# Planning a PE order with latencies and durations as traced per kind of matmul, and grouping PV by where the exponential was computed

## The chip, the cores and the metric

One core of one Trainium2 chip. The metric is the device time of one execution in microseconds. Most executions of a kernel agree within 0.3%; some fall into a slower state with a lower granted TensorE clock. Those are listed and left out of every comparison. Ratios are the mean time of one kernel's fast runs over that of the other's fast runs of the same rounds, so they are not quite the ratio of the medians that are quoted. The classes are faster, same and slower, with the line at 2%.

## The reference

Two attentions over the same sequence length, side by side in one program. Attention A is the heavy one: 16 query heads of width 28 share one key and one value head. Attention B looks back at 8 positions only.

```python
def _A_ref(x, wq, wk, wv, wo):           # x: 1 x 2048 x 448, H = 16, Dh = 28
    q = ...                               # x @ wq, split in 16 heads
    k = x @ wk; v = x @ wv                # one head each
    scores = jnp.einsum("bhqd,bkd->bhqk", q, k) * (Dh ** -0.5)
    p = _softmax(scores, axis=-1)         # 16 x 2048 x 2048 exponentials
    o = jnp.einsum("bhqk,bkd->bhqd", p, v)
    return ... @ wo

def _B_ref(x, wqkv, wo):                  # the same shapes; W = 8, dil = 2
    qkv = ...                             # x @ wqkv
    # keys and values at positions pos - 0, 2, ..., 14, with a mask
    logits = jnp.einsum("bhsd,bhswd->bhsw", q, kg) * scale
    attn = _softmax(...)
    return ... @ wo

return jnp.concatenate([a, b], axis=-1)
```

## The kernel before

ScalarE computes A's exponentials from PSUM, two or three score banks of 512 columns at a time (410 instructions). VectorE computes another 60 banks by a polynomial on the bits. TensorE (PE) makes the scores (QK), multiplies exponentials by values (PV), and fills what time is left with everything else: the projections of both attentions, B's logit sums and transposes, the output projections, and filler matmuls that are there to keep PE dense. QK and PV are *tiled*: two or three 32-row matmuls (QK) or four 32-column ones (PV) run side by side. The rest is called full-array work here; a projection over the 448 inputs takes three matmuls of 128 rows and one of 64. A second form of QK, called kz here, uses keys padded with zeros and the full array.

The kernel's order of instructions is not written down by hand. A greedy planner simulates the engines with a duration for each operation and latencies between engines, and emits each engine's list. What matters here is the rule that stops full-array work in time for the next QK. `H` is when ScalarE would run dry in the plan, `limit` is when PE must be free:

```python
class Sched:
    LAT = 0.13
    ...
    QKT = 0.32
    EPS = 0.03
    ...
        def ready(o):
            ...
                lat = self.LAT if d.eng != o.eng or d.dsem else (0.0 if o.eng == "pe" else self.OWN)
    ...
            H = tE["act"] + sum(o.dur for (_, o) in cand["act"] if o.ring)
            ...
            if e == "pe":
                rq = min((r for (r, o) in cand["pe"] if o.ring), default=None)
                if rq is not None and T > 14:
                    limit = max(rq, H - self.QKT - self.LAT)
                    ...
                    if limit is not None and not o.ring and T + o.dur > limit + self.EPS:
                        nxt = limit if nxt is None else min(nxt, max(limit, T + 0.02))
                        continue
```

And the way PV groups were formed. A PV group takes one bank from each of four heads. Banks that VectorE computes come late, and were put at the head of their list, so that they mixed with ScalarE's:

```python
            while late and late[0][0] <= n // 2:
                for x in late.pop(0)[1]:
                    quads[x[0][:2]][x[0][3]].insert(0, x)
            for u in us:
                js = quads[u[:2]]
                while all(js):
                    g.pv_group([x.pop(0) for x in js])
    ...
    def pv_group(self, grp):
        ...
        o = a("pe", 0.33, pv, ...)
        if last:
            o.deps.update(g.pvs[qd])
        elif not first:
            o.deps.add(g.pvs[qd][0])
```

Durations are constants or a rule: `t_mm(n) = 0.02 + 0.42e-3 * max(n, 100)`, which is 0.235 us for 512 columns.

## Time and profile before

| what | before |
|---|---|
| time, median of 3 runs | 475.45 us (475.41 to 476.12) |
| span of the profiled run, granted clock | 473.0 us, 0.999 |
| ScalarE busy | 451.8 us of 473.0 |
| first exponential starts, last ends | 12.31, 464.17 us |
| from the last exponential's end to the end | 8.8 us |
| waits between exponentials | 15.3 us |

How to read it: the page's busy share says which engine is full, and here it is ScalarE. The last row is not from the page. It is counted from the starts of the exponentials in the trace, as the prediction below works out.

### The profile page before, as it was taken

How to read it: one execution, taken by the hardware profiler on the slowest of the kernel's cores; microseconds unless marked ns; L12 is line 12 of the kernel's file. 1: busy time of each engine (PE TensorE's matmuls, PEld its weight loads, DVE VectorE, ACT ScalarE, POOL GpSimd, SP SyncE). 2: the span in 40 equal slices, each digit the busy share in tenths (PEclk: the TensorE clock that was granted, in tenths of full speed). 3: DMA queues.
4: the chain of work that ended last, by engine and by line, in shares of the span. 5: the costliest groups of instructions: out<-in, count | busy, mean ns of one | idle time of the engine just before them, and what ended most of it. 6: DMA issues, size and time to landing. Idle time of an engine off the chain costs nothing.

```text
span 473.0 us, 8630 instructions
## 1 busy us (share of the span) xinstructions
PE 436.5 (92%) x3629; PEld 173.3 (37%) x3684; DVE 365.2 (77%) x600; ACT 451.8 (96%) x430; POOL 12.5 (3%) x30
## 2 busy tenths in 40 slices
PE   8999999999899999999999999999999899989886
PEld 3433233343343424333343334322443244424333
DVE  4454878987888887897959688788968968786864
ACT  3999999999999999999999999999999999999993
POOL 8100000000000000000000000000000000000000
PEclk9999999999999999999999999999999999999999
DMA  9790022000220302000320302000310123013001
GB/s 193 147 219 3 2 87 89 11 1 10 80 89 21 108 29 89 11 10 2 98 79 30 108 14 86 10 11 15 111 63 11 50 79 97 12 48 119 11 0 60
DMA packets 41718, 27.34 MB, mean 58 GB/s; under 512 B 17090, under 2 KB 41520, under 8 KB 41680
## 3 DMA queue, kind: packets, MB, share of 16 engines
q1 hardware_dynamic: 39600, 25.25, 18.4%
q10 hardware_dynamic: 1776, 0.81, 0.7%
q0 software_dynamic: 304, 0.73, 0.6%
q8 instruction: 29, 0.48, 0.4%
q14 instruction: 9, 0.07, 0.1%
HBM read 17.60 MB, written 5.52 MB: 49 GB/s over the span
## 4 chain that ended last, share of the span: by engine, by line
ACT 70%; PE 26%; DVE 1%; DMA 1%; issue 1%; ACTq 0%
ACT expT L785 69%; PE ps L768 6%; PE ps L936 6%; PE ps L813 4%; PE ps L714 2%; PE ps L766 2%; PE ps L952 2%; DMA d_x<-in_A_wq_dram 1%; PE ps L643 1%; ACT e_t L1013 1%; PE ps L895 1%; PE ps L678 1%; PE ps L413 1%; PE ps L1045 1%; PE ps L728 0%
## 5 line engine op out<-in xcount | busy, mean ns | idle before, releaser
L785 ACT ACTIVATE expT<-ps 128x1024 bf16<-128x1024 f32 (+1 forms) x410 | 444.3, 1213 | 6.0 <-PE ps L768 4.5
L768 PE MATMUL ps<-qT,kT 32*128 32x512 bf16 x800 | 118.7, 384 | 14.5 <-ACT expT L785 11.2
L813 PE MATMUL ps<-expT,v_aug 128*32 128x512 bf16 x964 | 99.3, 389 | 0.1
L846 DVE TENSOR_SCALAR d_x<-ps 128x512 f32<-128x512 f32 x60 | 41.5, 691 | 45.2 <-PE ps L768 39.2
L766 PE MATMUL ps<-qT,kz 128*128 128x512 bf16 x189 | 58.6, 382 | 12.1 <-ACT expT L785 8.5
L768 PEld LDWEIGHTS ps<-qT,kT 32*128 32x128 bf16 x800 | 29.2, 90 | 80.8 <-ACT expT L785 51.8
L1038 PE MATMUL ps<-ident,prod 128*112 128x128 bf16 x512 | 48.5, 226 | 0.2 <-issue 0.2
L813 PEld LDWEIGHTS ps<-expT,v_aug 128*32 128x32 bf16 x964 | 24.9, 93 | 61.6 <-issue 58.1
L1038 PEld LDWEIGHTS ps<-ident,prod 128*112 128x112 bf16 x512 | 36.7, 129 | 21.8 <-issue 17.9
L936 PE MATMUL ps<-xT_B,wqkv 128*112 128x512 bf16 (+1 forms) x128 | 44.1, 407 | 0.2
L978 DVE TENSOR_TENSOR stage<-qTB,kTB 112x1024 bf16<-112x1024 bf16 x64 | 42.2, 679 | 2.2 <-PE ps L987 2.1
L1032 DVE TENSOR_TENSOR prod<-Vsh,a_n 128x896 bf16<-128x896 bf16 x64 | 37.4, 615 | 4.5 <-PE ps L1038 4.4
L858 DVE SCALAR_TENSOR_TENSOR dexp<-d_u,d_x 128x1024 int16<-128x1024 f32 x30 | 36.5, 1217 | 0.1
L856 DVE SCALAR_TENSOR_TENSOR d_u<-d_u,d_x 128x1024 f32<-128x1024 f32 x30 | 36.4, 1213 | 0.1
L854 DVE SCALAR_TENSOR_TENSOR d_u<-d_x 128x1024 f32<-128x1024 uint16 x30 | 36.3, 1210 | 0.1
L987 PEld LDWEIGHTS ps<-ones,stage 112*128 112x128 bf16 x512 | 20.4, 96 | 12.7 <-issue 7.6
L987 PE MATMUL ps<-ones,stage 112*128 112x4 bf16 x512 | 24.6, 167 | 0.1
L766 PEld LDWEIGHTS ps<-qT,kz 128*128 128x128 bf16 x224 | 14.3, 97 | 27.0 <-ACT expT L785 22.2
L936 PEld LDWEIGHTS ps<-xT_B,wqkv 128*112 128x112 bf16 (+1 forms) x128 | 14.2, 127 | 22.5 <-issue 18.3
L714 PE MATMUL ps<-xT_A,wq 128*128 128x512 bf16 (+1 forms) x60 | 19.9, 385 | 1.3 <-DVE v_aug L693 0.6
L952 PE MATMUL ps<-wqv,xT_B 128*128 128x448 bf16 x64 | 19.4, 358 | 0.0
L1045 PE MATMUL ps<-wo_B,oT 112*128 112x448 bf16 x64 | 18.1, 356 | 0.8 <-DVE oT L1041 0.8
(101 smaller groups left out, 310.2 us busy)
## 6 DMA issues: line engine op xcount, KB each, us to landing
Vsh<-v_scratch SPq DMA_DIRECT2D x16, 896.0 KB, 4.7
v_scratch<-Vst SPq DMA_DIRECT2D x16, 112.0 KB, 1.7
out_dram<-outB SPq DMA_DIRECT2D x16, 112.0 KB, 1.7
out_dram<-outA SPq DMA_DIRECT2D x14, 112.0 KB, 1.7
wqkv<-in_B_wqkv_dram SPq DMA_DIRECT2D x1, 672.0 KB, 4.7
stage<-in_A_x_dram ACTq DMA_DIRECT2D x1, 448.0 KB, 3.4
wo_B<-in_B_wo_dram SPq DMA_DIRECT2D x4, 98.0 KB
wo<-in_A_wo_dram SPq DMA_DIRECT2D x4, 98.0 KB
```

The costliest lines, as they stand in the source:

```text
L766: r = e.matmul(g.bank(b0 + i), g.kz[:, j, 128 * tb:128 * tb + 128], g.qT[:, sc % 2, t, :], start=True, stop=True)
L768: r = e.matmul(g.bank(b0 + i), g.kT[32 * j:32 * j + 32, 128 * tb:128 * tb + 128], g.qT[32 * j:32 * j + 32, sc % 2, t, :], start=True, stop ...
L785: x = a("act", t_exp(w), lambda e, b0=b0, w=w, n=n: e.activation(g.expT[:, n % ERING, 0:w], g.ps[:, 512 * b0:512 * b0 + w], ACT.Exp, scale ...
L813: x = e.matmul(g.bank(PVBANK, p0=32 * j, p1=32 * j + 32), g.v_aug[:, w, tb, :], src, start=first, stop=last, tile_position=(0, 32 * j))
L846: o = a("dve", t_dve_ps(512), lambda e: e.tensor_scalar(out=xx[:, 512 * h:512 * h + 512], in0=g.bank(bank), scalar1=-128.0 * A2, scalar2=1 ...
L856: a("dve", t_dve_1x(1024), lambda e: e.scalar_tensor_tensor(out=v, in0=u, scalar=EQ * F * F, in1=lo, op0=ALU.add, op1=ALU.mult), R=["d_u"] ...
L858: a("dve", t_dve_1x(1024), lambda e: e.scalar_tensor_tensor(out=out, in0=v, scalar=EL / F ** 3, in1=xx, op0=ALU.mult, op1=ALU.subtract), R ...
L936: a("pe", t_mm(512), lambda e, u=u, t=t, kt=kt, w=w: e.matmul(g.bank(u.bank, p1=KC), g.wqkv[64 * (kt // 3):, kt, w * D + KC * t:w * D + KC ...
L978: op = a("dve", t_dve_2x(1024), lambda e, t=t, qv=qv, kv=kv: e.tensor_tensor(out=g.prodT[0:KC, t, :, :], in0=qv, in1=kv, op=ALU.mult), R=R ...
L987: r = e.matmul(g.bank(u.bank, 128).rearrange("p (h w) -> p h w", w=WIN)[:, 4 * t:4 * t + 4, w], g.prodT[0:KC, t, w, :], g.ones4[:, :], sta ...
L1032: a("dve", t_dve_2x(2 * D), lambda e, qr=qr, Vv=Vv, av=av: e.tensor_tensor(out=g.prod2[:, 2 * qr:2 * qr + 2, :].rearrange("p w (d h) -> p ...
L1038: a("pe", 0.09, lambda e, u=u, t=t, w=w: e.matmul(g.bank(u.bank, 128, 128 * t, p1=KC), g.prod2[:, w, KC * t:KC * t + KC], g.ident[:, :], s ...
```

## The change

Its intent: let the planner know what the trace shows. One latency of 0.13 becomes one per engine. A switch from full-array to tiled work costs 0.09 us and is reserved. QK and PV are 0.315 us, four logit sums 0.1 instead of 0.2, a transpose 0.056 instead of 0.09. The 512-column projections keep 0.235. Four banks of VectorE form a PV group of their own, and the 16 groups of a quad may run in any order.

```diff
+    LATS = {"pe": 0.12, "act": 0.18, "dve": 0.08}
+    MODE = 0.09
+    NPV = 3
-    QKT = 0.32
+    QKT = 0.315
...
+    def lat(self, d):
+        if d.dsem or d.eng not in self.LATS:
+            return self.LAT
+        return self.LATS[d.eng] + (self.MODE if d.eng == "pe" and not d.tiled else 0)
...
-                    limit = max(rq, H - self.QKT - self.LAT)
+                    limit = max(rq, H - self.QKT - 0.12)
...
-                    if limit is not None and not o.ring and T + o.dur > limit + self.EPS:
+                    if limit is not None and not o.ring and not (o.pv and npv > self.NPV) and T + o.dur > limit + self.EPS - (0 if o.tiled else self.MODE):
...
-                elif (o.full and area(T) < (self.FULL[o.full] if T + 0.03 + 0.216 * o.full + self.LAT <= H + self.EPS else self.LOW)
+                elif (o.full and area(T) < (self.FULL[o.full] if T + 0.22 * o.full + 0.2 <= H + self.EPS else self.LOW)
...
+                if o.tiled and not mode:
+                    o.dur += self.MODE
+                mode = o.tiled
...
-                    quads[x[0][:2]][x[0][3]].insert(0, x)
+                    dqs[x[0][:2]][x[0][3]].append(x)
+                    if all(dqs[x[0][:2]]):
+                        g.pv_group([y.pop(0) for y in dqs[x[0][:2]]])
...
-        o = a("pe", 0.33, pv, ...)
-        if last:
-            o.deps.update(g.pvs[qd])
-        elif not first:
-            o.deps.add(g.pvs[qd][0])
+        o = a("pe", 0.315, pv, ...)
+        o.deps.update(g.evacs)
...
-                a("pe", 0.2, lgs, ...)
+                a("pe", 0.1, lgs, ...)
...
-                a("pe", 0.09, lambda e, u=u, t=t, w=w: e.matmul(
+                a("pe", 0.056, lambda e, u=u, t=t, w=w: e.matmul(
```

(Cut: the new fields of an operation, the same latencies used at bank releases and evacuations and in the limits for VectorE's work and for filler, kz planned at 0.22 us for each bank, and a table of offload positions that is rewritten with the same values.)

More of the change, by code (lines that the diff above doesn't have):

```diff
@@ L38 @@
 A2 = SCALE * 1.4426950408889634
-OFF_AT = {q: (0, 2, 4, 6, 7, 9) if q == 99 and q < 15 else (0, 2, 5, 7) for q in range(1, 16)}
+OFF_AT = {q: (0, 2, 5, 7) for q in range(1, 16)}
+OFF_AT.update({q: (0, 1, 3, 4, 6, 7, 9, 10) for q in ()})
 LATE = 2
@@ L50 @@
                  "kids", "start", "end", "seq", "waits", "signal", "count", "vc", "ninc", "claims", "idx",
-                 "dense", "fill", "full", "opt", "alone", "lock", "ring")
+                 "dense", "fill", "full", "opt", "alone", "lock", "ring", "tiled", "pv")
     def __init__(self, eng, dur, emit, pr, rel, name):
@@ L71, in __init__ @@
         self.ring = False
+        self.tiled = False
+        self.pv = False
         self.lock = isinstance(dur, Lock) or (eng == "gp" and emit is not None)
@@ L144, in run @@
         recent = []
+        mode = False
         locks = {"dve": 0.0, "gp": 0.0}
@@ L152, in ready @@
             for d in o.deps:
-                lat = self.LAT if d.eng != o.eng or d.dsem else (0.0 if o.eng == "pe" else self.OWN)
+                lat = self.lat(d) if d.eng != o.eng or d.dsem else (0.0 if o.eng == "pe" else self.OWN)
                 t = max(t, d.end + lat)
@@ L166, in use_ready @@
                         return None
-                    t = max(t, d.end + self.LAT)
+                    t = max(t, d.end + self.lat(d))
             return t
@@ L183, in run @@
                     n = sum(1 for (_, o) in cand["act"] if o.ring)
-                    limit = max(r1, H + (0.9 if n < 1 else 0) - self.QKT - 2 * self.LAT - 0.69)
+                    limit = max(r1, H + (0.9 if n < 1 else 0) - self.QKT - 0.2 - 0.69)
             if e == "pe":
@@ L187, in run @@
                 if rq is not None and T > 14:
-                    limit = max(rq, H - self.QKT - self.LAT)
+                    limit = max(rq, H - self.QKT - 0.12)
+            npv = sum(1 for (r, o) in cand[e] if o.pv and r <= T) if e == "pe" else 0
             for (r, o) in cand[e]:
@@ L254, in run @@
                     o.dense += 512 - o.use.spare
-                elif (o.full and area(T) < (self.FULL[o.full] if T + 0.03 + 0.216 * o.full + self.LAT <= H + self.EPS else self.LOW)
-                      and all(d.start is not None and d.end + self.LAT <= T for d in o.opt)):
+                elif (o.full and area(T) < (self.FULL[o.full] if T + 0.22 * o.full + 0.2 <= H + self.EPS else self.LOW)
+                      and all(d.start is not None and d.end + self.lat(d) <= T for d in o.opt)):
                     o.deps.update(o.opt)
-                    o.dur = 0.03 + 0.216 * o.full
+                    o.dur = 0.22 * o.full
+                    o.tiled = False
                     o.dense = 512 * o.full
@@ L263, in run @@
                     if T > 14 and area(T) > self.LOW:
-                        o.fill = max(0, min(o.fill, int((H - self.LAT - T - o.dur + self.EPS) / 0.22)))
+                        o.fill = max(0, min(o.fill, int((H - 0.12 - self.MODE - T - o.dur + self.EPS) / 0.22)))
                     o.dur += 0.22 * o.fill
                     o.dense += 512 * o.fill
+                if o.tiled and not mode:
+                    o.dur += self.MODE
+                mode = o.tiled
                 if o.dense:
@@ L286, in run @@
                     self.bank_last[b] = set(o.use.ops)
-                    self.bank_free_t[b] = max(x.end for x in o.use.ops) + self.LAT
+                    self.bank_free_t[b] = max(x.end + self.lat(x) for x in o.use.ops)
             for k in o.kids:
@@ L744, in a_loop @@
         assert len(units) == NU
-        g.last_exp, g.pvs = {}, {}
+        g.last_exp, g.pvs, g.evacs = {}, {}, []
         quads = {(sc, t): [[] for _ in range(4)] for sc in range(4) for t in range(4)}
+        dqs = {k: [[] for _ in range(4)] for k in quads}
         pair, late = [], []
@@ L771, in a_loop @@
             box = []
-            o = a("pe", 0.32, lambda e, qk=qk, box=box: qk(e, box=box), R=[("kT", tb // 4) for (_, _, tb, _) in us] + [("qT", sc % 2, t) for (sc, t, _, _) in us],
+            o = a("pe", 0.315, lambda e, qk=qk, box=box: qk(e, box=box), R=[("kT", tb // 4) for (_, _, tb, _) in us] + [("qT", sc % 2, t) for (sc, t, _, _) in us],
                   W=[("ring", slot)], pr=-50)
             box.append(o)
-            o.ring = True
+            o.ring = o.tiled = True
             o.full = len(us) if len(us) > 1 else 0
@@ L807, in pv_group @@
         qd = grp[0][0][:2]
-        n = len(g.pvs.setdefault(qd, []))
-        first, last = n == 0, n == 15
+        all_pv = g.pvs.setdefault(qd, [])
+        box = []
         def pv(e):
+            order = [o.seq for o in all_pv]
+            first, last = box[0].seq == min(order), box[0].seq == max(order)
             for (_, _, tb, j), _, src, w in grp:
@@ L815, in pv @@
             return x
-        o = a("pe", 0.33, pv, R=sorted({y[1] for y in grp}) + sorted(
-            {(k, y[3], y[0][2] // 4) for k in ("v_aug", "v_aug1") for y in grp}), W=["pv"] if first or last else [], pr=-40, dense=700)
-        if len(g.pvs) == 1 and first:
-            o.claims = [PVBANK]
-        if last:
-            o.deps.update(g.pvs[qd])
-        elif not first:
-            o.deps.add(g.pvs[qd][0])
-        g.pvs[qd].append(o)
-        if last:
+        o = a("pe", 0.315, pv, R=sorted({y[1] for y in grp}) + sorted(
+            {(k, y[3], y[0][2] // 4) for k in ("v_aug", "v_aug1") for y in grp}), pr=-40, dense=700)
+        o.tiled = o.pv = True
+        box.append(o)
+        if qd == (0, 0):
+            o.claims = [PVBANK]
+        o.deps.update(g.evacs)
+        all_pv.append(o)
+        if len(all_pv) == 16:
             g.a_quad_end(*qd)
@@ L866, in a_quad_end @@
         last = sc == 3 and t == 3
+        evacs = []
         hv = 2 if last else 1
@@ L873, in a_quad_end @@
             p0 = -30 if last else -1
-            a("dve", t_dve_ps(w), lambda e, cs=cs: e.transpose(out=g.PV_T[:, t % 2, cs], in_=g.bank(PVBANK)[:, cs]),
-              R=["pv"], W=kk("PV"), pr=-30)
+            o = a("dve", t_dve_ps(w), lambda e, cs=cs: e.transpose(out=g.PV_T[:, t % 2, cs], in_=g.bank(PVBANK)[:, cs]),
+                  W=kk("PV"), pr=-30)
+            o.deps.update(g.pvs[sc, t])
+            evacs.append(o)
             pt = g.PV_T[:, t % 2, :].rearrange("p (b e) -> p b e", e=32)
@@ L884, in a_quad_end @@
               R=[("oN", x) for x in keys], W=[("oTn", t, x) for x in keys], pr=p0)
+        g.evacs = evacs
         pr = end + 20
@@ L989, in lgs @@
                     return r
-                a("pe", 0.2, lgs, R=[("prodT", t), "ones4"], W=[u], use=u, pr=pr)
+                a("pe", 0.1, lgs, R=[("prodT", t), "ones4"], W=[u], use=u, pr=pr)
         par = (k // 2) % 2
```

## The prediction

> **What bounds the kernel now.** The page's busy times first, then the exponential's row by shape, then the chain of waits in order of time, then single starts in the trace.
>
> ```profile
> PE 436.5 (92%) x3629; PEld 173.3 (37%) x3684; DVE 365.2 (77%) x600; ACT 451.8 (96%) x430; POOL 12.5 (3%) x30
> ...
> ACT 70%; PE 26%; DVE 1%; DMA 1%; issue 1%; ACTq 0%
> ...
> L785 ACT ACTIVATE expT<-ps 128x1024 bf16<-128x1024 f32 (+1 forms) x410 | 444.3, 1213 | 6.0 <-PE ps L768 4.5
> ```
>
> ScalarE is the bound: 410 exponentials of two or three score banks. The page gives only 6.0 us of idle before them, which would cap any gain at 1.3%. That figure is too small. A waiting exponential overlaps the tail of the one before, so part of each wait is inside "busy". The chain of waits shows it better:
>
> ```profile
> 110.12 1.49 PE ps L936 x5
> 112.93 1.27 PE ps L936 x4
> 114.58 31.11 ACT expT L785 x29
> ...
> 446.52 12.65 ACT expT L785 x12
> ```
>
> Where only ScalarE is on the chain it makes 12 exponentials in 12.65 us, 1.054 each. From starts in the trace, the undisturbed step is 1.331 us after a three-bank exponential (145 of them) and 0.904 us after a two-bank one (264): 145 x 1.331 + 264 x 0.904 + one short = 432.1 us. The 8 small exponentials of the other attention take 0.43 each (3.4) and the 4 column ones about 0.1 each. The phase runs from 12.31 to 464.17, 451.9 us, so some **15.3 us** are waits. PE pieces as above stand in the chain wherever the next scores came late.
>
> Taking each start minus the one before minus its undisturbed step, I sorted the 15.3 us by what stood ahead of the score matmuls (QK): 9.6 us in 54 waits where a tiled QK stood behind full-array work (6.5 of it behind the projections wqkv and wq); 2.0 us in 13 waits at triples of the untiled form of QK (kz); 2.0 us in 11 waits where QK was ready and the exponential waited for something else; 0.4 us at kz pairs; 1.3 us in scatter below 25 ns. The two largest of the 2.0 us, at 88 and 97 us (0.64 and 0.81), are a full ring of exponentials: PV groups that contain a VectorE bank were held until VectorE's last step ended at 97.53, and QK stood behind PV.
>
> **The time budget of one QK.** After a two-bank exponential PE has 0.904 us. The trace has 0.171 us from its end to the QK that reuses its banks, and 0.442 us from that QK's start to the next exponential: 0.613 us, so 0.29 us is left for whatever PE is still doing.
>
> ```profile
> 459.22 0.39 PE L763 MATMUL ps<-warm 128*128 128x512 bf16 x1 [0.23 <-ACT expT L785]
> 459.54 0.39 PE L768 MATMUL ps<-qT,kT 32*128 32x512 bf16 x3
> 459.86 0.40 PE L813 MATMUL ps<-expT,v_aug 128*32 128x512 bf16 x4
> 460.19 0.61 PE L766 MATMUL ps<-qT,kz 128*128 128x512 bf16 x2
> ```
>
> Starts differ by 0.32 for each tiled group and 0.32 for a full-array matmul before QK, though full-array matmuls follow each other at 0.216 to 0.227. So a switch into a tiled mode costs about 0.09 us.
>
> **What the Trainium skill says.** (1) "TensorEngine Tiling (Array Packing)", Tiling Modes, Key Properties: changing the tiling mode drains TensorE. The trace agrees: 0.322 for filler to QK against 0.22 filler to filler; 0.285 for the output projection to QK against 0.189 within it. (2) "TensorE: Matmul & The Clock Gate", Single matmul latency: (398 + N) / 2.4 ns warm, 379 ns at N = 512; the trace has 384 to 389. Granted clock is 0.999, so the clock gate plays no part before. (3) "ScalarE: Activation LUTs", What ACT_TABLE_LOAD costs (its paragraph on ACTIVATE): 186 ns + 0.833 N, back-to-back ones overlapping by about 93 ns, hence 946 ns at N = 1024; the trace steps at 904, and that is used. (4) "Perfetto Trace Analysis", Identifying the Most-Contended Engine: occupancy is a fair measure for ScalarE, not for TensorE. Here 96% hides a third wait in "busy", so I used starts.
>
> **The change, part by part.** No exponential, bank, matmul of the result or offload is added or removed; the orders give the same 410 exponentials with 60 banks on VectorE. Only the planner's numbers change, and the grouping of PV.
>
> *Latencies and the switch.* Before, the planner let full-array work run to 0.13 + 0.32 = 0.45 us before ScalarE would run dry, with one latency of 0.13 each way: 0.58 in all, and no switch. Measured are 0.613 and 0.09 on top, so each filled gap is short by 0.12. The new numbers are 0.18 + 0.315 + 0.12 = 0.615 and 0.09, which is what the trace shows. Of the 9.6 us, 5.3 lie within the first 0.12 us of the waits and should go. The other 4.3 us come from projections: the planner takes 0.235 for a 512-column matmul, and that is not changed; the trace has 0.26 to 0.31 for wqkv and 0.225 to 0.32 for wq, 0.03 to 0.08 too little each. They sit ahead of 83 tiled QKs in the new order against 69. But gaps are filled in steps of 0.235, so most have room for 0.03 to 0.1. Estimate: 2.7 of 9.6 us stay; **-6.9**.
>
> *kz triples.* A triple takes 3 x 0.226 and ends 0.862 us after its start; with 0.171 that is 1.03 against 0.904, hence the 0.13 us each. The planner now asks 0.22 x 3 + 0.2 = 0.86, and the orders show triples fall from 14 to 4. **-1.4** of 2.0.
>
> *VectorE's four banks as one group.* One PV group in 16 waits for VectorE instead of up to four mixed ones, and exponentials' buffers no longer hang on it. **-1.5** of 2.0. Pairs and scatter stay (1.7).
>
> *The end.* The last block of the other attention closes the kernel:
>
> ```profile
> 466.05 1.00 PE ps L1038 x18
> 467.06 0.82 PE ps L895 x4
> 467.88 0.61 DVE outA L905
> 468.49 0.67 DVE oT L1041
> 469.21 0.94 PE ps L1045 x4
> ```
>
> After the last QK the order had 29 of its transposes, the new one 9; at 0.056 us these are 1.1 us. They now all precede the last output matmuls, and oT is evacuated before outA instead of after both, so the final block starts about 0.6 x 2 earlier. **-1.1**.
>
> *The head, which gets worse.*
>
> ```profile
> 0.81 15.57 SPq L578 DMA_TRANSPOSE xT_A<-in_A_x_dram  x12
> ...
> 11.94 0.35 PE ps L768 x3
> 12.31 1.46 ACT expT L785
> ```
>
> The first QK waits for nothing but k and q. The old order had ten key projections ahead of it, the last needing the sixth transpose. The new one has twelve, the last two needing the seventh and eighth. Transposes are issued 1.30 us apart, so the eighth goes out at 9.9 and, by its landing record, is in at 13.58. The first QK must follow: 13.58 + 0.06 + 0.31 for that matmul = 13.95 instead of 11.94. The first exponential moves from 12.31 to about 14.3: **+2.0**, and as ScalarE is the bound all of it counts. The planner believes in faster transposes (0.9 us apart).
>
> Sum: -6.9 - 1.4 - 1.5 - 1.1 + 2.0 = -8.9, so 475.45 - 8.9 = **466.5 us**, -1.9%.
>
> **The rivals.** (a) *Only the page's idle counts* (6.0 us): 475.45 - 6.0 - 1.1 + 2.0 = 470.4. For it: that is what the profile prints. Against: the starts, where 49 waits of over 0.1 us follow two-bank exponentials alone. (b) *The projections take the wait over*: with their 0.235 unchanged and 83 instead of 69 of them ahead of QK, the 4.3 us stay whole and some new waits come: 468 to 470. For it: more QKs sit right behind them (57 for wqkv against 45). Against: the 0.09 is now kept free at each. (c) *PE becomes the bound.* Adding the traced steps over the new order gives 409 us of PE work from first to last QK against 432 of exponentials (411 in the old one); PE isn't the bound on average, but with 95% load a stricter limit can push PV back until the seven exponential buffers are full. 4 us of that would make it 470. (d) *All waits go and the head is harmless*: 475.45 - 14 - 1.1 = 460.
>
> **Range and chances.** The head (+2.0) and the end (-1.1) are read from the orders and sure to about 0.5. The waits left are the wide term: 5.4 of 15.3 expected, 2.5 to 10 plausible. That gives 462.0 to 471.5 around 466.5. The 2% line is at 465.9 and lies 0.6 us under the centre, so faster and same are near even, same a little ahead. Slower would need a new stall of 18 us, of which nothing speaks but an unforeseen dependency or a lost clock: 0.02.
>
> **What would show it.** The first exponential at about 14.3 us behind a wait for the transpose: head right; at 12.3: wrong. Exponentials: steps over 0.904 and 1.331 summing to 3 to 7 us, the rest behind wqkv and wq; if the sum stays over 10, the latencies were not the cause or (b) or (c) holds. No exponential with QK ready and a long wait: the grouping worked. From the last exponential to the end 7.7 us instead of 8.8. PEclk must stay at 9 in all slices; a slice lower makes the prediction wrong, and so does an idle PE that waits for VectorE's four-bank group.

## The result, and the profile after

| | before | after |
|---|---|---|
| fast runs, first batch | 475.31 to 476.12 us (4) | 469.65, 468.96 us |
| slow runs | none | 477.92, 478.23 us (clock 0.974, 0.975) |
| median of all 4 | 475.43 us | 473.78 us |
| ratio of fast runs, 95% interval | | 0.9868 (0.9844 to 0.9892): same |

The fast runs are 6.1 us shorter. The profiled run after is a fast one, so the two traces compare. The page of the changed kernel, its busy row, its chain of waits by engine, and the exponentials' row (busy and mean ns, then idle before them):

```profile
span 467.6 us, 8711 instructions
PE 441.1 (94%) x3700; PEld 171.0 (37%) x3700; DVE 363.5 (78%) x600; ACT 449.7 (96%) x430; POOL 12.8 (3%) x30
ACT 68%; PE 28%; SPq 1%; DMA 1%; DVE 1%; issue 0%
L804 ACT ACTIVATE expT<-ps 128x1024 bf16<-128x1024 f32 (+1 forms) x410 | 441.8, 1211 | 3.9 <-PE ps L787 3.4
```

ScalarE is still the bound and still 96% busy. Its idle time before exponentials fell by 2.1 us and its busy time by 2.1; neither figure is the 6.0 us by which the waits fell, counted below. The chain's PE share did not fall, 26% before and 28% now. That is the first sign that many waits are still there, only shorter.

Where the 5.4 us of span went, from starts in the two traces:

| | before | after | difference |
|---|---|---|---|
| first exponential starts | 12.31 | 14.68 | +2.4 |
| first exponential to end of last | 451.9 | 445.4 | -6.5 |
| end of last exponential to end of kernel | 8.8 | 7.6 | -1.2 |

The waits between exponentials, sorted as in the prediction (us, and in brackets how many waits of over 25 ns):

| the exponential waits because | before | predicted | after |
|---|---|---|---|
| tiled QK stood behind full-array work | 9.6 (54) | 2.7 | 6.2 (64) |
| tiled QK stood behind tiled work | 0 | 0 | 0.6 (4) |
| kz triple | 2.0 (13) | 0.6 | 0.4 (2) |
| kz pair | 0.4 (5) | 0.4 | 0.3 (5) |
| scores ready, exponential waits for something else | 2.0 (11) | 0.5 | 0.3 (8) |
| scatter below 25 ns | 1.3 | 1.3 | 1.4 |
| sum | 15.3 | 5.5 | 9.2 |

Every row but the first did what was predicted, to 0.6 us. The first gave 3.4 of the expected 6.9.

One thing is missing from this count: the waits beside the four small column operations that ScalarE runs between exponentials. Before, there are two, 0.6 us in all (at 17 and 29 us, both behind full-array work); after, none of note. With them the sums are about 15.9 and 9.3 us, and the fall of 6.6 us fits the 6.5 us that the phase lost. In later tables e6 and e12 lack 1.4 us each for the same reason, e7 and e10 0.3.

This stretch of the chain of waits, in order of time (start, length, what), shows the head of the changed kernel:

```profile
5.99 1.26 SPq L596
7.29 5.89 DMA xT_A<-in_A_x_dram
13.18 0.05 issue
13.23 1.08 PE ps L661 x3
14.31 0.53 PE ps L787 x5
```

The first QK (L787) comes directly after three key projections (L661) that had waited for a transposed load. And the end, from the same view:

```profile
459.12 1.24 PE ps L921 x6
460.36 0.36 PE ps L836 x4
...
462.81 0.76 PE ps L921 x3
...
464.11 0.60 DVE outA L931
464.72 0.59 DVE outB L1074
```

B's transposes and the copy of their result, which stood between A's last PV and the last output before, are gone from it.

What remains in the middle looks like this in PE's timeline (start, length, operation, shapes, count):

```profile
47.27 0.39 PE L787 MATMUL ps<-qT,kT 32*128 32x512 bf16 x2
47.59 1.21 PE L962 MATMUL ps<-xT_B,wqkv 128*112 128x512 bf16 x4
48.72 0.39 PE L787 MATMUL ps<-qT,kT 32*128 32x512 bf16 x3
```

Four projections hold PE from 47.59 to the QK at 48.72, that is 1.13 us. The plan had 4 x 0.235 + 0.09 = 1.03. The exponential of that QK came 0.14 us late. So the switch is reserved now, but the projections overrun it.

The experiments below treat this as one matter of the projections' duration. The starts in the trace say more: from each of the four to what follows it takes 0.260, 0.216, 0.309 and 0.352 us. The last of the four has 64 rows, and the step from a 128-row to a 64-row matmul costs about 0.09 us as well (0.309 against 0.216 here; 0.285 against 0.189 for the 448 columns of wqv). It is a second switch, and the plan reserves only the one into tiled work. Of the 3.4 us of waits behind wqkv and wq, 2.4 (18 waits) follow projections with such a 64-row matmul among them and 1.0 (12 waits) follow projections without one, though the QKs of the two sorts are about as many (42 and 41). No run plans this switch by itself.

### The profile page after: what moved, and what is told of

Same layout as the page of the kernel before. It is cut to its first block, busy times and chain, and to the rows that moved or that the text cites. A ratio compares the mean times of both kernels' runs of the same rounds, so it can differ in the third digit from the quotient of the medians.

```text
span 467.6 us, 8711 instructions
## 1 busy us (share of the span) xinstructions
PE 441.1 (94%) x3700; PEld 171.0 (37%) x3700; DVE 363.5 (78%) x600; ACT 449.7 (96%) x430; POOL 12.8 (3%) x30
## 4 chain that ended last, share of the span: by engine, by line
ACT 68%; PE 28%; SPq 1%; DMA 1%; DVE 1%; issue 0%
ACT expT L804 67%; PE ps L787 6%; PE ps L836 5%; PE ps L962 4%; PE ps L785 2%; PE ps L1064 2%; SPq L596 1%; DMA xT_A<-in_A_x_dram 1%; PE ps L732 1%; PE ps L921 1%; PE ps L431 1%; PE ps L978 1%; PE ps L696 1%; ACT e_t L1039 1%; PE ps L1013 1%; PE ps L661 0%
## 5 line engine op out<-in xcount | busy, mean ns | idle before, releaser
L787 PE MATMUL ps<-qT,kT 32*128 32x512 bf16 x838 | 124.3, 384 | 9.9 <-ACT expT L804 8.1
L836 PE MATMUL ps<-expT,v_aug 128*32 128x512 bf16 x964 | 95.9, 389 | 1.0 <-ACT expT L804 1.0
L787 PEld LDWEIGHTS ps<-qT,kT 32*128 32x128 bf16 x838 | 30.6, 91 | 84.3 <-ACT expT L804 58.9
L785 PE MATMUL ps<-qT,kz 128*128 128x512 bf16 x186 | 55.6, 382 | 4.7 <-ACT expT L804 4.6
L1064 PE MATMUL ps<-ident,prod 128*112 128x128 bf16 x512 | 43.8, 224 | 0.1
L1064 PEld LDWEIGHTS ps<-ident,prod 128*112 128x112 bf16 x512 | 34.8, 129 | 16.7 <-issue 12.7
L732 PE MATMUL ps<-xT_A,wq 128*128 128x512 bf16 x64 | 21.3, 386 | 0.5 <-DVE qT L755 0.5
L1013 PEld LDWEIGHTS ps<-ones,stage 112*128 112x128 bf16 x512 | 18.0, 96 | 7.6 <-issue 3.6
L1013 PE MATMUL ps<-ones,stage 112*128 112x4 bf16 x512 | 20.7, 167 | 0.0
L785 PEld LDWEIGHTS ps<-qT,kz 128*128 128x128 bf16 x186 | 12.1, 98 | 20.7 <-ACT expT L804 18.3
```

The lines of the kernel that those rows point to most:

```text
L785: r = e.matmul(g.bank(b0 + i), g.kz[:, j, 128 * tb:128 * tb + 128], g.qT[:, sc % 2, t, :], start=True, stop=True)
L787: r = e.matmul(g.bank(b0 + i), g.kT[32 * j:32 * j + 32, 128 * tb:128 * tb + 128], g.qT[32 * j:32 * j + 32, sc % 2, t, :], start=True, stop ...
L836: x = e.matmul(g.bank(PVBANK, p0=32 * j, p1=32 * j + 32), g.v_aug[:, w, tb, :], src, start=first, stop=last, tile_position=(0, 32 * j))
L1013: r = e.matmul(g.bank(u.bank, 128).rearrange("p (h w) -> p h w", w=WIN)[:, 4 * t:4 * t + 4, w], g.prodT[0:KC, t, w, :], g.ones4[:, :], sta ...
L1064: a("pe", 0.056, lambda e, u=u, t=t, w=w: e.matmul(g.bank(u.bank, 128, 128 * t, p1=KC), g.prod2[:, w, KC * t:KC * t + KC], g.ident[:, :], ...
```

## The experiments

Each edit is against the changed kernel. All results were correct. The kernel before ran beside them on each chip, at 475.48 to 475.62 us median. Three theories were to be told apart. *Spacing*: what remains is where the plan's durations are shorter than the trace's. *Head*: what is missing was lost in the first 15 us. *Reshuffle*: a different order is a different draw, and differences of a microsecond mean nothing.

### e1_head: the head alone undone

Only four key projections are moved, behind the third group of scores; nothing else changes place.

```diff
+    def k2_later(self):
+        pe = s.seqs["pe"]
+        k2 = [o for o in pe if o.use is not None and o.use.name == "K2"][:4]
+        ring = [o for o in pe if o.ring]
+        rest = [o for o in pe if o not in k2]
+        n = rest.index(ring[2]) + 1
+        s.seqs["pe"] = rest[:n] + k2 + rest[n:]
+        # (cut: positions and start times made consistent)
```

> The changed kernel with only the four key projections of chunk 2 moved behind the third group of scores; every other instruction keeps its place. Theory (the head waits for a transposed load): the first exponential comes at 12.2 to 12.5 us instead of 14.68, and all of the 2.3 us stays saved to the end, so 466.5 to 467.3 in the fast state. Rival (the head is harmless, the time is made up for later, or the score wait only moves to the next exponential): the time stays within 0.6 us of the changed kernel's fast 469.3.

Measured: 468.75, 468.48, 468.77 us fast, one slow at 477.51; ratio 0.9855. Their mean of 468.7 is 0.6 us under the changed kernel's 469.3, not 2. The profiled run was a slow one, so its times are not compared with others, but the order of events is read. VectorE's timeline there (the last bracket is the idle time before, and what ended it):

```profile
12.12 0.42 DVE L701 TENSOR_TENSOR d_u<-kT 128x512 bf16<-128x512 bf16 x1
16.89 0.69 DVE L699 CAST kT<-ps 128x512 bf16<-128x512 f32 x1 [4.35 <-PE ps L689]
```

VectorE's next instruction was the copy of exactly those four projections, so it sat 4.35 us (in this slow run; in a fast one that time is not known) and the keys behind it came late. The first exponential was earlier, the following ones waited. The head theory falls as it was put: the 2.4 us at the first exponential are not 2.4 us at the end. The traces of before and after say the same: by the 17th exponential the changed kernel is only 0.7 us behind (32.91 against 32.21), because the kernel before had 1.5 us of waits in its first 40 us (2.0 with those beside the column operations) and the changed one 0.3. But e1 brings a wait of its own, so it does not tell what a late first exponential costs when nothing else changes; e9 below does.

### e2_numbers_only and e3_grouping_only: the two halves of the change

e2 keeps the new numbers and takes the old PV grouping; e3 the other way round.

```diff
 e2: -                    dqs[x[0][:2]][x[0][3]].append(x) ...
     +                    quads[x[0][:2]][x[0][3]].insert(0, x)       (and the old pv_group)
 e3: -    LATS = {"pe": 0.12, "act": 0.18, "dve": 0.08}; MODE = 0.09; QKT = 0.315 ...
     +    LATS = {}; MODE = 0.0; QKT = 0.32                            (and the old durations)
```

> The planner's new numbers with the old grouping of PV. It has the late head too (twelve key projections before the first scores) and no work of the other attention after the last scores. Theory (the two parts save different waits): waits of ready scores for a full ring come back, 1.5 us or more in a few waits of over 0.3 us, while waits behind full-array work stay near the changed kernel's 6.2 us; 470.5 to 473. Rival (the grouping does nothing of its own): 469 to 470 and no such wait.

> The new grouping of PV with the planner's old numbers. Its head is the old one (first exponential near 12.3 us). Theory: ring waits under 0.5 us instead of 2.0, but waits behind full-array work at 9 to 11 us and at kz triples 1.5 to 2.5 us as before; 472 to 474.5. Rival (the grouping is the whole gain and the numbers do nothing): 467 or less. On the slow state: this order has 238 untiled score matmuls against 186 in the changed kernel; if slow runs come from a lower granted clock where the array is less filled, none of its runs is slow.

Measured: e2 471.93 to 472.22 us (3 fast, 3 slow at 480.14 to 495.13), ratio 0.9926 (0.9912 to 0.9941). e3 473.22 to 474.04 us (5 fast, 1 slow at 489.07), ratio 0.9957 (0.9944 to 0.9971). Times 475.5 these are -3.5 and -2.0 us. Both times lie in the ranges of their theories. Together -5.5, against -6.3 for both at once (1 - 0.9868): nearly additive. Both profiled runs were slow ones, so the waits that the theories name could not be read, and e3's slow run contradicts its guess on the slow state. The grouping is worth about what the prediction gave it (-1.5); the numbers are what fell short.

### e5_changed_again: the changed kernel, unchanged, in a later batch

> The changed kernel as it is, to have its fast time and its share of slow runs beside the next three on one chip. Fast runs near 469.3; one to four of six slow, at 477 to 480, and if a slow one is profiled, its clock is halved in one block of time that begins between 10 and 20 us and nowhere else. Rival for the slow state: the halved clock is spread over the kernel.

Measured: 469.41, 468.66, 469.0 us fast; 491.27, 478.03, 477.69 us slow; ratio 0.9858 (0.9841 to 0.9875). The trace sorts into the same classes to 0.01 us (6.22 us in 64 waits behind full-array work). So these waits came out the same in two runs of one order, and can be argued about one by one.

### e9_control: a reshuffle that means nothing

```diff
-    EPS = 0.03
+    EPS = 0.031
```

> The changed kernel with the planner's margin moved by a nanosecond (0.030 to 0.031 us): a control for what a mere reshuffle of the order is worth. Reshuffle theory (the gains of the wider margin and of the longer projections are luck of the order): 467.0 to 471.0 us, that is, it differs from the changed kernel's 469.0 by over 0.8 us one way or the other, and waits behind full-array work move by over 1.5 us from 6.2. Spacing theory (they are gains from planning what the trace shows): 468.5 to 469.8 us, and behind full-array work 5.5 to 7.0 us.

Measured: 468.19 and 469.01 us fast, 478.18 and 476.34 slow; ratio 0.9855 (0.9837 to 0.9873). Behind full-array work 6.0 us in 60 waits. The waits moved by 0.2 us, as spacing has it; the mean of the two runs, 468.6, is 0.4 us from 469.0, though the lower run is 0.3 us under spacing's range. As a control it is weak: the nanosecond hardly changed the order. What stands ahead of a score matmul is the same as in the changed kernel for 1001 of 1024 (for e7 for 530), and nearly all of the rest lies between 299 and 326 us. So what a real reshuffle is worth was not measured, and reshuffle stays open for differences of a microsecond between e4, e7, e10 and e11.

The trace of the lower run shows something else: the same three key projections stood before the first QK, but the transposed loads landed earlier (the eighth at 12.77 us, not 13.79) and its first exponential started at 13.57 us instead of 14.68. So the head itself varies by 1.1 us from run to run. And with the order so nearly equal, those 1.1 us were kept: the 17th exponential starts at 31.79 instead of 32.91, and the last ends at 458.54 instead of 460.04.

### e4_margin and e7_proj: what is left, reserved in two ways

e4 keeps 0.13 us more free ahead of every QK. e7 plans the 512-column projections with a spacing like the traced one.

```diff
 e4: -    EPS = 0.03
     +    EPS = -0.10
 e7: -    return 0.02 + 0.42e-3 * max(n, 100)
     +    return {512: 0.265, 448: 0.208}.get(n, 0.02 + 0.42e-3 * max(n, 100))
```

> The changed kernel with the planner told to end work 0.13 us earlier ahead of each group of scores (EPS from 0.03 to -0.10). Theory (the remaining 6.2 us of waits behind full-array work are the projections' and other steps that run 0.03 to 0.1 us longer than planned, and lateness carried over): these waits fall to 2 to 3.5 us, the time to 465 to 467.5. Rival (PE is the bound; what is kept free ahead of the scores is missing elsewhere): waits move to other kinds and the sum stays at 8 us or more, 468 to 471.

> The changed kernel with 0.265 instead of 0.235 us planned for every 512-column full-array matmul (448 columns stay at 0.208). Theory (half of the waits left are these matmuls running longer than planned): waits behind projections fall from 3.4 to 1.5 us or less, those behind other work stay; the planner itself now leaves 1.2 us more of gaps, so 467 to 469.3. Rival (the waits are lateness that is carried over from earlier work, whatever stands last): the waits behind projections stay above 2.5 us.

Measured: e4 467.49 to 470.4 us in 5 runs, ratio 0.9857 (0.9837 to 0.9876); behind full-array work 4.3 us in 48 waits, but kz triples are back at 2.4 us. Its theory (2 to 3.5 us, 465 to 467.5) missed, but for the lowest run's time; the sum of waits is still some 8 us and the other four runs lie at 468 to 471, as its rival said. Its two longest runs, 469.53 and 470.4, show clocks of 0.996 and 0.993. e7 467.49 to 467.68 us in 4 runs, ratio 0.9831 (0.9818 to 0.9844); behind full-array work 3.65 us in 45 waits. Behind the projections wqkv and wq it is 1.3 us where the changed kernel has 3.4. The exponentials' row and the chain of e7:

```profile
ACT 72%; PE 22%; DVE 2%; SPq 2%; DMA 1%; issue 0%
L804 ACT ACTIVATE expT<-ps 128x1024 bf16<-128x1024 f32 (+1 forms) x410 | 441.9, 1226 | 2.0 <-PE ps L787 1.2
```

The idle time before exponentials halves, from 3.9 to 2.0, and PE's part in the chain falls from 28% to 22%. So the waits behind the projections are a matter of their planned duration. (0.265 is an average that covers the 64-row step too.) But the sum of waits falls only from 9.2 to 8.3: kz triples and pairs come back with 3.0 us where the changed kernel has 0.8. And of the 1.5 us that e7 gains over e5, only 0.6 lie between the first exponential and the last (444.8 against 445.3); the rest is an earlier head (13.37 against 14.63): this order has 11 key projections ahead of the first QK, not 12.

### e6_mode0 and e12_mode0_old_short: is it the switch?

e6 takes the switch away and leaves all other new numbers. e12 does the same, and also plans the two short kinds as long as before.

```diff
 e6 and e12: -    MODE = 0.09
             +    MODE = 0.0
 e12 too:    -                a("pe", 0.1, lgs, ...
             +                a("pe", 0.2, lgs, ...
             -                a("pe", 0.056, lambda e, u=u, t=t, w=w: e.matmul(
             +                a("pe", 0.09, lambda e, u=u, t=t, w=w: e.matmul(
```

> The changed kernel with the planner's cost of a switch into a tiled mode set to zero (MODE 0.09 to 0), its latencies kept. Theory (the switch is most of what was missing: 0.09 of 0.12): waits behind full-array work go back up from 6.2 to 9 us or more, mean wait from about 0.10 to about 0.17 us, fast time 471 to 474 although its head is early. Rival (the latencies did it, the switch matters little): waits behind full-array work stay at 5.5 to 7, and with the early head the time is 467.5 to 469.

> The run without the switch (MODE 0, 478.2 us) once more, but with the two short kinds of full-array matmul planned as long as before: 0.09 us for a transpose of the other attention and 0.2 for a group of four logit sums, where the trace has 0.056 and 4 x 0.025. Theory that the old over-long durations had kept the room that the switch needs: waits of scores behind these two kinds fall from 3.4 us (23 waits) to under 1, waits behind full-array work in all from 14.4 to 9 to 12 us, time 473.5 to 476 us. Rival, that without the switch the other new latencies are what costs: waits behind the projections and fillers stay, the short kinds don't matter, and the time stays at 477 to 479 us.

Measured: e6 478.16 to 478.34 us (4 fast, one slow at 489.83), ratio 1.0056 (1.0042 to 1.0069). It is slower than the kernel before, and 4 us over its theory's range: the sign was foreseen, the size was not. e12 471.5 to 472.31 us in 4 runs, ratio 0.9927 (0.991 to 0.9944), 1.2 to 2.0 us better than its theory's range and far from the rival's. The chain of waits of e6, by engine and by line, then of e12:

```profile
PE 50%; ACT 46%; SPq 1%; DMA 1%; DVE 1%; issue 0%
ACT expT L804 45%; PE ps L787 12%; PE ps L836 8%; PE ps L962 6%; PE ps L1064 6%; PE ps L785 4%; PE ps L732 3%; PE ps L978 2%; PE ps L1013 2%; PE ps L431 1%; PE ps L1071 1%; SPq L596 1%; DMA xT_A<-in_A_x_dram 1%; PE ps L408 1%; PE ps L696 1%; PE ps L746 1%
```

```profile
ACT 75%; PE 21%; SPq 1%; DMA 1%; DVE 1%; issue 1%
ACT expT L804 74%; PE ps L787 5%; PE ps L962 5%; PE ps L836 3%; PE ps L732 2%; SPq L596 1%; PE ps L785 1%; DMA xT_A<-in_A_x_dram 1%; PE ps L978 1%; ACT e_t L1039 1%; PE ps L431 1%; PE ps L696 1%; PE ps L921 0%; PE ps L661 0%; PE ps L703 0%
```

In e6 the transposes (L1064, 6%) and logit sums (L1013, 2%) are on the chain, in e12 neither is. What stood ahead of the waiting QK, in us:

| tiled QK behind | before | changed | e6 | e12 | e7 | e10 |
|---|---|---|---|---|---|---|
| projections wqkv, wq | 6.5 | 3.4 | 6.9 | 6.4 | 1.3 | 1.0 |
| projection wqv | 1.0 | 0.3 | 1.1 | 1.5 | 0.6 | 0.1 |
| filler | 1.5 | 0.6 | 1.3 | 1.1 | 0.5 | 0.0 |
| transposes, logit sums, output projections | 0.4 | 1.9 | 4.6 | 0.4 | 1.1 | 2.0 |
| all full-array work (with smaller kinds) | 9.6 | 6.2 | 14.4 | 9.6 | 3.65 | 3.3 |

e12 has the latencies per engine and the right QK and PV durations, but neither the switch nor the right short kinds, and its 9.6 us are the 9.6 us of before. So without the switch and the short kinds the new numbers took nothing off this class. e6 adds the right short kinds and loses 4.8 us in it, 4.2 of them in the last sort of the table: 3.3 behind transposes and logit sums, the rest behind output projections. The changed kernel adds the switch and gains 8.2.

This is what the prediction had not seen: the old, too long durations of the short kinds had been a reserve. The planner left off early there, and those kinds stood almost never just ahead of a waiting QK (three waits, 0.4 us). With true durations they fill the gap to the brim, and each of them then brings a switch. The change paid for that with its own new constant.

### e8_dense_head: more filler in the first 45 us

The slow runs of e1 to e3 show the clock halved for a block that begins at 14 to 17 us (e1's row of granted clock, in tenths):

```profile
PEclk9559999999999999999999999999999999999999
```

e8 asks for more filler there.

```diff
+    def more(self, T):
+        return 300.0 if T < 45 else 0.0
-            ... and area(T) < self.IDLE):
+            ... and area(T) < self.IDLE + self.more(T)):
```

> The changed kernel with the planner's wanted filling of the array 300 columns per us higher in the first 45 us (25% more filler there). Theory (the slow state is the clock halved at the head because the array is filled too little there): no run of six is slow and all clocks are 0.995 or more; the fast time is the same or up to 1.5 us longer, 469 to 471. Rival (the slow state has nothing to do with the filling): slow runs as often as in the changed kernel.

Measured: 470.68 to 476.6 us in 6 runs with clocks of 0.985 to 1.0; ratio 0.9965 (0.9935 to 0.9995). None was classed as slow, but four of the six still show a clock below 0.995, and the fastest is 1.4 us worse than the changed kernel's fast mean of 469.3. A miss: more filler doesn't settle it, and costs time. Of the changed kernel and orders close to it (e1, e5, e9) 8 of 18 runs were slow; of the kernel before 3 of 34; of e2, e3 and e6 5 of 17; of e4, e7, e10, e11 and e12 none of 24. What in the order decides this stays open.

### e10_proj_margin and e11_combined: the best of these together

```diff
 e10: -    EPS = 0.03
      +    EPS = -0.02                         (and e7's duration)
 e11: -    EPS = 0.03
      +    EPS = -0.06
      -    a("sp", 0.9, ... dma_start(... transpose=True)), ... land=2.5
      +    a("sp", 1.3, ... dma_start(... transpose=True)), ... land=3.3
      +    HB = g.HB if c == 0 else g.LB if c == 1 else (6, 7)      (and likewise for V)
```

> Projections of 512 columns planned at 0.265 us and the margin at -0.02 us as well. Spacing theory: the waits left behind full-array work in the run with longer projections (3.65 us) are under the scatter of a start, so the margin takes about 1 us off them and 0.5 off the kz pairs and triples, while the planner itself plans 0.5 us more of gaps: 466.3 to 467.6 us, at or a little under the 467.6 of longer projections alone. Reshuffle theory: anywhere from 466 to 470 us.

> The margin at -0.06 us, the transposed loads planned as traced (1.3 us from issue to issue, 3.3 to land), and the copies of later K and V chunks moved to other PSUM banks, so that the head is planned without the surprise that cost the changed kernel its first microseconds. Spacing theory: behind full-array work about 4.5 us as with the wider margin, first exponential at 13.3 to 14.0 us, 466.5 to 468.2 us. If the head is set by the transposed loads' own landing whatever is planned: first exponential at 14.3 to 14.8 us and 467.5 to 468.8 us.

Measured: e10 466.58 to 466.78 us in 5 runs, ratio 0.9814 (0.9801 to 0.9826): the best of all, still classed the same, with the 2% line inside its interval. e11 467.1 to 467.83 us in 6 runs, ratio 0.9831 (0.9819 to 0.9844): the range of spacing holds for the time, but not its way. First exponential at 12.09 us, earlier than both theories said, and 2.4 us of waits in the first 40 us give it back, one of 1.7 behind a key projection; behind full-array work 6.95 us. As in e1, the head's gain is not kept. The page of e10:

```profile
ACT 82%; PE 14%; SPq 1%; DMA 1%; DVE 1%; issue 0%
L804 ACT ACTIVATE expT<-ps 128x1024 bf16<-128x1024 f32 (+1 forms) x410 | 441.6, 1262 | 1.7 <-PE ps L787 1.2
L785 PE MATMUL ps<-qT,kz 128*128 128x512 bf16 x201 | 59.8, 383 | 4.8 <-ACT expT L804 4.4
```

PE's part of the chain is 14%, half of the changed kernel's. 7.5 us of waits remain: 3.3 behind full-array work, 2.7 at kz triples and pairs, which are more in number again (201 matmuls against 186), and 1.4 others.

## Why the prediction was right or wrong

**The bound and the method** held. ScalarE stayed the bound, and the sum of starts, not the page's idle, was the right measure: idle fell by 2.1 us, the time by 6.1. Its own terms give 451.9 - 432.1 - 3.4 - 0.4 = 16.0 us of waits, where it sorts 15.3: the difference is mostly the two waits beside column operations.

**The time** was 469.3 us (mean of the two fast runs) for 466.5 predicted, inside the range of 462.0 to 471.5. The class is the one that had the most weight. That the time fell inside the range is owed to its width: the largest term came to half of what it was put at. The sum of waits left, 9.2 us, is outside the 3 to 7 that it named as the sign of being right. The gain was 6.1 us instead of 8.9, and the table tells which terms made the difference:

| term | predicted | measured |
|---|---|---|
| waits behind full-array work | -6.9 | -3.4, and +0.6 new behind tiled work |
| kz triples | -1.4 | -1.6 |
| ring waits, from the grouping | -1.5 | -1.6 (e3 alone: -2.0 with its other effects) |
| the end | -1.1 | -1.2 |
| the head | +2.0 | +2.4 at the first exponential |
| waits beside column operations, in no other row | 0 | -0.6 |

The measured terms sum to -5.4 us, the difference of the two profiled spans.

**The step that failed** is this one: "Of the 9.6 us, 5.3 lie within the first 0.12 us of the waits and should go", with "Estimate: 2.7 of 9.6 us stay". The mechanism, that a gap is planned too full by the switch, was right: without the switch the same kernel takes 478.2 us (e6). The size was not. 6.2 us stay, for two reasons that the runs show. First, 3.4 us behind wqkv and wq and 0.3 behind wqv against the 2.7 that were to be all; the mean wait of the class fell from 0.18 to 0.10 us while their number rose from 54 to 64. The prediction's "most have room for 0.03 to 0.1" was not so: planning them at 0.265 takes 2.1 us of the 3.4 away (e7). It read their spacing as 0.26 to 0.31 and 0.225 to 0.32, but did not see that the upper ends are the 64-row matmul, a switch of its own, behind which 2.4 of the 3.4 us stand. Second, 1.9 us in 23 waits behind transposes and logit sums (1.2) and output projections (0.7), which the prediction didn't count because there had been 0.4 us in three. It treated the changed durations of the short kinds as harmless, and they had been hiding the switch (e6 against e12). And not all of the 3.4 us that went is the numbers' doing: some 1.0 of it lies in the first 40 us, where the order of the head differs.

**The head** was right as a chain (first QK behind key projections behind a transposed load, 14.31 us) and 0.4 us too low for the first exponential, within the 1.1 us by which e9 shows that this moves between runs. "As ScalarE is the bound all of it counts" holds for a delay alone (e9: 1.1 us at the first exponential are 1.1 at the 17th and still there at the end). It was wrong for this change, because the old order paid for its early start with waits that the new one has not: by the 17th exponential 0.7 us of the 2.4 are left, and undoing the head gave 0.6 us (e1: 468.7 against 469.3).

**The ring.** The full ring at 88 and 97 us fits the trace, and these two waits are gone. "QK stood behind PV" is not what the trace shows. ScalarE's list has exponentials exchanged there: scores that QK made at 86.30 us were used at 88.98, and ScalarE first waited for a QK that could start only at 87.62, when its banks came free at 87.55; at 97 us it is the same with the scores of 96.30 and a kz pair at 96.99.

**The rivals.** (b), the projections take the wait over, 468 to 470 us, names the right time, which the prediction's centre misses by 2.8 us, and half of the reason. It expected the 4.3 us beyond the first 0.12 to stay whole; in fact that part fell to 1.2 and the small waits stayed, 5.0 us against 5.3 before. (a) is close in time (470.4) by a wrong reason. (c), PE as the bound through a full ring, is refuted: exponentials with scores ready wait 0.3 us in all. (d) is far off.

**What would have shown it wrong**: the granted clock at 9 in all slices held in fast runs; in half of the runs of this kernel it did not, which the chance of a slow result was not meant for.

## What to carry to other kernels

When a planner's constants are corrected from a trace, correct them all or expect the corrected ones to expose the rest: a duration that was too long may be the reserve for a cost that isn't modelled. Count waits from starts and sort them by what stood ahead, before and after; the number and mean of each sort tell whether a cause went or only shrank. Look for a modelled cost in every kind that can bring it: here the switch was planned for tiled work alone, and the 64-row matmul has it too. And a delay at the head counts only so far as the work behind it would not have waited anyway.

## What the Trainium skill lacked or had wrong

- "TensorEngine Tiling (Array Packing)", Tiling Modes, Key Properties, says that a change of mode drains TensorE, and gives no size. Here it adds about 0.09 us from start to start: transpose to QK 0.152 against 0.056 between transposes, output projection to QK 0.285 against 0.189, logit sum to QK 0.098 against 0.025. A 64-row matmul after a 128-row one has it too, 0.309 against 0.216. Left out of a plan with otherwise true durations it cost 9 us (478.2 against 469.3).
- "TensorE: Matmul & The Clock Gate", Part 1, has the clock halve after an idle window of some 3.4 us (3413 ns). In the slow runs of e1, e2 and e3 the half clock lasts 23.9, 20.5 and 41.0 us, by that figure 7, 6 and 12 windows, from 14 to 17 us on, where the busy row of PE shows nine tenths. The changed kernel's slow runs are 8.6 to 22 us longer than its fast ones, 1.8 to 4.7%. Why a PE that looks busy is throttled there no run shows.
- The same page, Weight-path perf modes, ties fast weight loads to 128 weights. The trace agrees as far as loads go: 126 ns for 112 columns (wqkv) and 98 ns for 128 (kz). What neither it nor another page has is a spacing for loads of under 128 columns: wqkv matmuls of 512 columns start 0.260 us apart in 22 of 34 pairs and 0.216 in the other 12, where the others take 0.216 to 0.227. That the slower load is the reason is not shown. The plan's 0.235 misses this and, more, the 64-row step.
- No page has a measured issue time of a transposed load on this chip (the one figure that there is, a cycle count for earlier generations, stands in a part on trn3): they leave 1.3 us apart here, 1.23 to 1.26 us each on the queue, and in the changed kernel the eighth, landing at 13.79 us, sets when the first scores can start.
